# The tile that two attention heads share: three operand pairs for its scores where there were four, with copies inside SBUF

## The chip, the cores and the metric

The kernel runs on one core of a Trainium2 chip. The metric is the device time of one execution, in microseconds (us). The engines are named as in the profile: PE multiplies matrices (PEld is its loading of the stationary operand), DVE, ACT and POOL work on elements, and SP only issues transfers, which the core's DMA engines then carry out.

## The reference, cut to what matters

Three layers follow one another. The first is attention over 16 heads (2 batches of 8) of 1152 keys and 64 features; the queries are averaged in pairs, so a head has 576 of them:

```python
q_pool = q.reshape(B, H, S // 2, 2, D).mean(axis=3)
scores = scale * q_pool @ k.T
attn = softmax(scores)          # over the 1152 keys
x = attn @ v
```

Two feed-forward layers come after it (512 to 2048 to 512 with ELU; an RMS norm, and 512 to 1536 to 512 with SwiGLU). The change touches only the scores of the first layer.

## The kernel before, in words

All matrix products are made in a type that keeps fewer bits than float32, so every operand is split in an upper part (the value rounded to that type) and a lower part (what the rounding left), and a product is a sum over such parts. For the scores this is laid out along the 128 rows that a product sums over. A head has 64 features. Its keys are in a tile `kd` of 128 x 1152: rows 0 to 63 hold the upper parts of the 64 features, rows 64 to 127 the lower parts (`prep_k`, L248). Its queries are in a tile `qt` of 128 x 2 x 704: plane 0 has the upper parts, in both halves of the rows, plane 1 the lower parts, in both halves too (`prep_q`, L236). So plane 0 times `kd` gives upper times (upper plus lower), and plane 1 times `kd` gives lower times (upper plus lower). The first and last 64 columns of `qt` are zeros.

The heads are worked in 8 pairs, p = 0 to 7, with j = 0 and 1 in a pair. A head's 576 queries are four tiles of 128 and a rest of 64. The rests of both heads make one shared tile, number 2 (`M`) in the list `TILES`, so that a pair has nine tiles. In the shared tile the first 64 output rows belong to one head and the last 64 to the other, and the zero columns of `qt` keep the heads apart.

The loop over `steps` has 72 steps, one for each tile: `emit_S` (L268) makes the scores in PSUM (tile `s`, one buffer of three banks, each written by products of 384 columns) and DVE reads them once (L283) into `p`, with their extreme; `do_T` transposes the tile of two steps ago on PE (L297), with ACT (L305) and DVE (L69) splitting the result into `pth` and `ptl`; `do_AV` runs eight products with the values (L323); `emit_exp` is on ACT (L288). A full tile takes 2 operand pairs x 3 banks = 6 score products, the shared tile 4 x 3 = 12. The order within a pair is the list's, so the shared tile is the third; only pair 0 has it fifth.

Each engine works through its instructions in the order in which the program gives them, and so does SP's queue of transfers. Behind the exponent a step has up to one preparing job for the heads of the next pair (`plan`, L401): a job waits for a raw load (`load`, L221, tiles `rawq`, one buffer, and `rawk` and `rawv`, two buffers together), and POOL adds the query pairs, rounds and subtracts (L243, L60, L63). When a job is emitted, the load for the job after it is put in SP's queue (`fetch`, L396). In pair 0 ACT does some of the rounding (L389). In the last 33 steps a step also puts out one operation on the weights of the next layer (`ws.step`, L500), whose loads (L90) are in SP's queue too. POOL also joins the halves of the output (L339) and spreads the softmax sums (`rs`).

Of the kernel before, what the change touches and what calls it, by code (L numbers as in the profile page):

```python
# [9 lines left out]
F32R = mybir.dt.float32r  # L10
# [8 lines left out]
S = 1152  # L19
# [19 lines left out]
def tile_kernel(ctx: ExitStack, tc: tile.TileContext, qd, kd, vd, w1d, w2d, wgd, wvd, wod, rgd, outd):  # L39
    nc = tc.nc  # L40
    V, G, T, PE, SP = nc.vector, nc.gpsimd, nc.scalar, nc.tensor, nc.sync
    ctx.enter_context(tc.manual_schedule())
    f = lambda a: a.bitcast(F32)
# [29 lines left out]
    class Stream:  # L73
# [10 lines left out]
        def load(self, n):  # L84
            while self.loaded < min(n, len(self.srcs)):
                i = self.loaded
                t = wp.tile([128, 512, 2], U32, tag="wr", name="wr", bufs=2)
                r = t.rearrange("p c w -> p (c w)")
                if wide:
                    SP.dma_start(out=r, in_=self.srcs[i].bitcast(U32))  # L90
                else:
                    t = f(r)[:, 0:512]
                    SP.dma_start(out=t, in_=self.srcs[i])
                self.raw[i] = t
                self.loaded += 1
# [103 lines left out]
    ap = actx.enter_context(tc.tile_pool(name="attn", bufs=1))  # L199
# [19 lines left out]
    KD, VD, QD = {}, {}, {}  # L219
# [28 lines left out]
    def prep_k(p, j, half, t, eng):  # L248
# [4 lines left out]
        hi(d, t)  # L253
        lo(d[64:128], t[64:128], d[64:128])

    def prep_v(p, j, t, eng):
        hi, lo = eng
        d = VD[p, j] = ap.tile([128, 9, 128], F32R, tag="vd", name="vd", bufs=3)
        hi(d[:, :, 0:64], t)
        lo(d[:, :, 64:128], t, d[:, :, 0:64])  # L260
# [7 lines left out]
    def emit_S(p, i):  # L268
        if i == 0:
            st[p] = ap.tile([128, 4, NPT, 1], F32, tag="st", name="st", bufs=2)  # L270
        s = (tp if (p, i) == (0, 1) else sp).tile([128, 3, 512], F32, tag="s", name="s", bufs=1)
        if i == M:
            parts = [(QD[p, j][:, u, c:c + 128], KD[p, j]) for j, c in ((1, 0), (0, 576)) for u in (0, 1)]
        else:
            j, c, _, _, _ = TILES[i]
            parts = [(QD[p, j][:, u, c:c + 128], KD[p, j]) for u in (0, 1)]
        for n, (a, b) in enumerate(parts):
            for m in range(3):
                PE.matmul(s[:, m, 0:384], lhsT=a, rhs=b[:, 384 * m:384 * m + 384],  # L279
                          start=n == 0, stop=n == len(parts) - 1)  # L280
        pt = P[p, i] = ap.tile([128, 3, 384], F32, tag="p", name="p", bufs=3)

        V.tensor_scalar(out=pt, in0=s[:, :, 0:384], scalar1=-0.0625, scalar2=None,  # L283
                        op0=ALU.mult, op1=ALU.min, accum_out=st[p][:, 0, TILES[i][4], :])

    def emit_exp(p, i):
        pt = P[p, i]
        T.activation(out=pt, in_=pt, func=AF.Exp, scale=-1.0, bias=st[p][:, 0, TILES[i][4], :],  # L288
                     accum_out=st[p][:, 1, TILES[i][4], :])
# [57 lines left out]
    def emit_r(p):  # L347
        s = st[p]
        V.tensor_scalar(out=s[:, 2], in0=s[:, 1], scalar1=1e-9, scalar2=None, op0=ALU.add)
        V.reciprocal(s[:, 3], s[:, 2])  # L350
        hi_pool(rs, s[:, 3, 0:8].to_broadcast([128, 8, 64]))

    def emit_scale(p):

        s, x = st[p], xf[p]
        rb, rm = tbank(), tbank()
        for k in range(4):
            PE.transpose(rb[:, 128 * k:128 * k + 128], rs[:, 2 * k:2 * k + 2, :].rearrange("p a b -> p (a b)"), ident)
        PE.transpose(rm[:, 0:128], s[:, 3, 8, :].to_broadcast([128, 128]), ident)
        xs = ap.tile([128, QS], F32, tag="xs", name="xs", bufs=1)  # L360
        for a, b in ((0, 0), (320, 256)):
            T.copy(xs[:, a:a + 256], rb[:, b:b + 256])
        for j in range(2):
            r = slice(64 * j, 64 * j + 64)
            T.copy(xs[r, 256:320], rm[r, r])
        return xs

    def emit_x(p, xs, a=0, b=QS):
        x = xf[p][:, a:b]
        n, c = divmod(p, 4)  # L370
        h, l = (t[:, c, n * QS + a:n * QS + b] for t in (xh, xl))
        if p < 7:
            G.tensor_tensor(out=x, in0=x, in1=xs[:, a:b], op=ALU.mult)
            hi_pool(h, x)
            lo_pool(l, x, h)
        else:
            V.tensor_tensor(out=x, in0=x, in1=xs[:, a:b], op=ALU.mult)
            T.copy(h, x)
            lo_dve(l, x, h)
# [11 lines left out]
    def do_prep(u, eng):  # L391
        {"q": prep_q, "k": prep_k, "v": prep_v}[u[0]](*u[1:], raws.pop(u), eng)
# [3 lines left out]
    def fetch(u):  # L396
        if u not in raws:
            raws[u] = load(*u)


    plan = {1: lambda p: ("v", p, 0), 2: lambda p: ("q", p + 1, 1), 3: lambda p: ("k", p + 1, 1, 0),  # L401
            4: lambda p: ("k", p + 1, 1, 1), 5: lambda p: ("v", p + 1, 1), 6: lambda p: ("q", p + 1, 0),
            7: lambda p: ("k", p + 1, 0, 0), 8: lambda p: ("k", p + 1, 0, 1)}
    steps = [(p, i) for p in range(8) for i in ([0, 1, 3, 4, 2, 5, 6, 7, 8] if p == 0 else range(NPT))]
    ns = len(steps)
    jobs = {n: [] for n in range(-1, ns)}
    for n in range(ns):
        p, k = n // NPT, n % NPT
        if p == 0:
            u = {0: [("k", 0, 0, 1)], 2: [("v", 0, 1)], 3: [("v", 0, 0)]}.get(k, [])  # L410
            jobs[n] += u
        if k in plan and not (p == 0 and k == 1):
            u = plan[k](p)
# [36 lines left out]
    def do_T(step):  # L450
        pt, it = steps[step - LT]
        if avq and any(overwrites(it, a.g) for a in avq):
            assert not any(overwrites(it, a.g) for a in avq[1:])
            avq[0].emit(18)
        emit_T(pt, it)

    def do_AV(k, then):
        while k and avq:
            k -= avq[0].emit(k)
            if avq[0].n < 18:  # L460
                break
            a = avq.pop(0)
            a.finish()
            if a.g is GROUPS[3]:
                then(a.p)

    def after_T(step):
        pt, it = steps[step - LT]
        seen.add((pt, it))
        for g in GROUPS:  # L470
            if it in g["tiles"] and all((pt, t) in seen for t in g["tiles"]):
                avq.append(AV(pt, g))

    for step in range(ns):
        emit_S(*steps[step])
        if step == 1:
            tctx.close()
            tp = actx.enter_context(tc.tile_pool(name="psT", bufs=1, space=PSUM))
            tbank = lambda: tp.tile([128, 512], F32, tag="t", name="t", bufs=3)

        due = [w for w in later if w[0] <= step]
        if step >= LT and not due:
            do_T(step)
        for w in due:
            later.remove(w)
            w[1]()
        do_AV(8, lambda p: later.append((step + 2, lambda: emit_x(p, emit_scale(p)))))
        if step >= LT and due:
            do_T(step)
        emit_exp(*steps[step])  # L490
        if step >= LT:
            if steps[step - LT][1] == NPT - 1:
                emit_r(steps[step - LT][0])
            after_T(step)
        for u in jobs.get(step, []):
            do_prep(u, (ACT[0], lo_pool) if step < 4 and u[0] != "q" else POOL)
            n = order.index(u)
            if n + 1 < len(order):
                fetch(order[n + 1])
        ws.step(0, step >= ns - 33)  # L500


# [87 lines left out]
    for hf in range(2):  # L590
# [28 lines left out]
        if hf:  # L619
            T.activation(out=dummy, in_=eps, func=AF.Sqrt)  # L620
            for c in range(3):
                for n in range(4):
                    m, q = 2 + n // 2, n % 2
# [113 lines left out]
```

## Time and profile before

| | us |
|---|---|
| median of 3 runs | 697.13 (696.63 to 697.89) |
| the profiled execution: its own time | 696.5 |
| the profiled execution: span from first to last instruction | 694.7 |
| attention within the span | about 0 to 257 |
| PE busy, of the span | 680.0 (98%) |
| DVE busy | 538.2 (77%) |
| ACT busy | 415.0 (60%) |
| POOL busy | 372.6 (54%) |

The span is what the trace shows, and the execution's own time lies 1.8 us above it. Busy shares are means over stages of different make: in attention all five engines are used hard, in the two later layers PE above all. PE's busy time counts products that overlap each other, so 98% doesn't say that PE works at its peak.

### The profile page before, as it was taken

What the parts mean: (1) busy time and instruction counts of PE and PEld (TensorE: products, weight loads), DVE (VectorE), ACT (ScalarE), POOL (GpSimd) and SP (SyncE); (2) the same over time, 40 slices, a digit from 0 to 9 for tenths busy, and PEclk for the clock granted to TensorE, in tenths of its full rate; (3) what the DMA queues carried; (4) which work ended last, traced back from release to release, by engine and by line L of the source; (5) the groups of instructions that cost most, each with busy time, mean ns of one, the idle gap of its engine ahead of it and who ended that gap; (6) DMA issues with size and microseconds to landing.
All of it is one profiled execution on the core that took longest, in us unless ns stands there. A gap on an engine that the chain in (4) does not pass through costs nothing.

```text
span 694.7 us, 11366 instructions
## 1 busy us (share of the span) xinstructions
PE 680.0 (98%) x4243; PEld 668.1 (96%) x4243; DVE 538.2 (77%) x891; ACT 415.0 (60%) x855; POOL 372.6 (54%) x332
## 2 busy tenths in 40 slices
PE   7999999999999999999999999799999999999998
PEld 6999999989898999999999999799999999999997
DVE  6888889898999877999959999866999876584000
ACT  5888889789888857774447764334444443342000
POOL 5988788897978405674434544532554343342000
PEclk9999999999999999999999999999999999999999
DMA  5423323432432000213422123201323222232000
GB/s 181 144 86 113 128 87 103 144 119 87 134 129 72 1 31 32 92 60 129 145 92 85 67 86 127 91 1 38 116 92 121 92 97 92 87 106 80 35 35 34
DMA packets 21607, 62.34 MB, mean 90 GB/s; under 512 B 2736, under 2 KB 4784, under 8 KB 21552
## 3 DMA queue, kind: packets, MB, share of 16 engines
q1 hardware_dynamic: 21552, 61.62, 26.2%
q8 instruction: 33, 0.54, 0.3%
q14 instruction: 22, 0.18, 0.1%
HBM read 59.25 MB, written 2.36 MB: 89 GB/s over the span
## 4 chain that ended last, share of the span: by engine, by line
PE 78%; DVE 15%; ACT 4%; issue 1%; DVEq 0%; ACTq 0%
PE b L167 16%; PE b L169 16%; PE b L168 16%; PE s L279 10%; PE o L323 9%; PE t L297 8%; DVE p L283 3%; DVE ptl L69 2%; DVE wt L124 2%; DVE wt L128 2%; DVE wt L120 1%; DVE gl L69 1%; DVE e L187 1%; DVE wt L122 1%; ACT gh L188 1%
## 5 line engine op out<-in xcount | busy, mean ns | idle before, releaser
L167 PE MATMUL b<-xh,wh 128*128 128x384 f32 x468 | 157.3, 336 | 0.6 <-ACT sl L638 0.6
L169 PE MATMUL b<-xh,wl 128*128 128x384 f32 x468 | 157.1, 336 | 0.0
L168 PE MATMUL b<-xl,wh 128*128 128x384 f32 x468 | 157.0, 335 | 0.0
L63 POOL TENSOR_TENSOR wl<-wt,wh 128x512 fp32r<-128x512 f32 x68 | 98.4, 1447 | 76.6 <-ACT wh L141 48.2
L283 DVE TENSOR_SCALAR_CACHE_REDUCE p<-s 128x1152 f32<-128x1152 f32 x72 | 97.4, 1354 | 21.1 <-PE s L279 20.7
L69 DVE TENSOR_TENSOR ptl<-t,pth 128x384 fp32r<-128x384 f32 x216 | 106.7, 549 | 3.5 <-ACT pth L305 3.0
L279 PE MATMUL s<-kd,qt 128*128 128x384 f32 x480 | 98.0, 341 | 5.6 <-DVE p L283 4.6
L305 ACT CAST pth<-t 128x384 fp32r<-128x384 f32 x216 | 89.3, 486 | 23.1 <-PE t L297 22.5
L288 ACT ACTIVATE p<-p,st 128x1152 f32<-128x1152 f32 x72 | 91.4, 1269 | 5.2 <-DVE p L283 4.9
L279 PEld LDWEIGHTS s<-kd,qt 128*128 128x128 f32 x480 | 81.5, 188 | 9.0 <-DVE p L283 4.0
L167 PEld LDWEIGHTS b<-xh,wh 128*128 128x128 f32 x468 | 87.9, 188 | 0.9 <-ACT sl L638 0.9
L168 PEld LDWEIGHTS b<-xl,wh 128*128 128x128 f32 x468 | 87.9, 188 | 0.0
L169 PEld LDWEIGHTS b<-xh,wl 128*128 128x128 f32 x468 | 87.9, 188 | 0.0
L297 PE MATMUL t<-ident,p 128*128 128x128 f32 x648 | 85.9, 275 | 0.0
L323 PE MATMUL o<-pth,vd 128*128 128x256 f32 (+1 forms) x288 | 84.4, 315 | 0.0
L297 PEld LDWEIGHTS t<-ident,p 128*128 128x128 f32 x648 | 73.9, 141 | 6.8 <-DVE ptl L69 4.3
L323 PE MATMUL o<-ptl,vd 128*128 128x256 f32 (+1 forms) x288 | 78.4, 295 | 0.0
L113 ACT ACTIVATE wt<-wr 128x512 f32<-128x512 f32 x68 | 45.7, 672 | 51.2 <-POOL wl L63 31.8
L124 DVE SCALAR_TENSOR_TENSOR wt<-wr,wt 128x512 uint32<-128x512 uint32 x68 | 73.2, 1076 | 1.4
L128 DVE CUSTOM_DVE_ANT_0 wt<-wt,we 128x1024 uint16<-128x1024 uint16 x68 | 66.7, 981 | 1.9
L63 POOL TENSOR_TENSOR gl<-e,gh 128x384 fp32r<-128x384 f32 x37 | 40.2, 1087 | 44.5 <-ACT gh L188 42.8
L167 PE MATMUL b<-gh,wh 128*128 128x384 f32 x180 | 61.5, 342 | 0.0
(113 smaller groups left out, 1321.3 us busy)
## 6 DMA issues: line engine op xcount, KB each, us to landing
wr<-in_w_dram SPq DMA_DIRECT2D x32, 512.0 KB, 3.2
rawk<-in_k_dram SPq DMA_DIRECT2D x32, 288.0 KB, 2.9
rawq<-in_q_dram SPq DMA_DIRECT2D x15, 576.0 KB, 3.9
wr<-in_wg_dram SPq DMA_DIRECT2D x12, 512.0 KB, 3.2
wr<-in_wv_dram SPq DMA_DIRECT2D x12, 512.0 KB, 3.2
wr<-in_wo_dram SPq DMA_DIRECT2D x12, 512.0 KB, 3.2
rawv<-in_v_dram SPq DMA_DIRECT2D x16, 288.0 KB, 2.8
out_dram<-o SPq DMA_DIRECT2D x12, 192.0 KB, 1.8
```

The costliest lines, as they stand in the source:

```text
L63: G.tensor_tensor(out=o, in0=i, in1=f(h), op=ALU.subtract)
L69: V.tensor_tensor(out=o, in0=i, in1=f(h), op=ALU.subtract)
L124: V.scalar_tensor_tensor(out=t, in0=hi, scalar=0x80000000, in1=t, op0=ALU.bitwise_and, op1=ALU.bitwise_xor)
L167: PE.matmul(out, lhsT=wh[:, k, :], rhs=ah, start=first and k == 0, stop=False)
L168: PE.matmul(out, lhsT=wh[:, k, :], rhs=al, start=False, stop=False)
L169: PE.matmul(out, lhsT=wl[:, k, :], rhs=ah, start=False, stop=last and k == 3)
L279: PE.matmul(s[:, m, 0:384], lhsT=a, rhs=b[:, 384 * m:384 * m + 384], start=n == 0, stop=n == len(parts) - 1)
L283: V.tensor_scalar(out=pt, in0=s[:, :, 0:384], scalar1=-0.0625, scalar2=None, op0=ALU.mult, op1=ALU.min, accum_out=st[p][:, 0, TILES[i][4], :])
L288: T.activation(out=pt, in_=pt, func=AF.Exp, scale=-1.0, bias=st[p][:, 0, TILES[i][4], :], accum_out=st[p][:, 1, TILES[i][4], :])
L297: PE.transpose(ps[:, k, :], src[:, 128 * b:128 * b + 128], ident)
L305: T.copy(oh, re(ps))
L323: PE.matmul(self.o[:, 0:self.N], lhsT=v[:, b, :], rhs=(pth, ptl)[u][:, g["buf"], b, g["c0"]:320], start=self.n == 0, stop=self.n == 17)
```

## The change

For the shared tile, the two products with the lower parts of the queries, one for each head, become one. A new stationary tile `qm` (128 x 128) is block-diagonal: rows and columns 0 to 63 hold the lower parts of head 0's 64 queries, rows and columns 64 to 127 those of head 1's; the rest is set to zero once. A new moving tile `km` (128 x 1152) has the upper parts of head 0's keys in rows 0 to 63 and those of head 1's in rows 64 to 127. The shared tile then has three operand pairs, and nine products; the products of lower parts with lower parts are no longer in it.

`qm` and `km` have one buffer each and are filled for each pair by four transfers inside SBUF in SP's queue (`prep_m`): a 64 x 64 block into `qm` and 64 x 1152 into `km`, for either head. They are put out behind the job that prepares head 0's queries for the next pair (for pair 0, behind that of the second half of head 0's keys). The order of the jobs is changed: head 0's keys go to steps 5 and 6, its queries to step 7, and head 1's values from step 5 to step 8.

```diff
+    qm = ap.tile([128, 128], F32R, name="qm")
+    km = ap.tile([128, S], F32R, name="km")
+    V.memset(f(qm), 0.0)
+
+    def prep_m(p):
+        for j, c in ((0, 576), (1, 64)):
+            r = slice(64 * j, 64 * j + 64)
+            SP.dma_start(out=f(qm[r, r]), in_=f(QD[p, j][r, 1, c:c + 64]))
+            SP.dma_start(out=f(km[r]), in_=f(KD[p, j][0:64]))
...
         if i == M:
-            parts = [(QD[p, j][:, u, c:c + 128], KD[p, j]) for j, c in ((1, 0), (0, 576)) for u in (0, 1)]
+            parts = [*((QD[p, j][:, 0, c:c + 128], KD[p, j]) for j, c in ((1, 0), (0, 576))), (qm, km)]
...
     plan = {1: lambda p: ("v", p, 0), 2: lambda p: ("q", p + 1, 1), 3: lambda p: ("k", p + 1, 1, 0),
-            4: lambda p: ("k", p + 1, 1, 1), 5: lambda p: ("v", p + 1, 1), 6: lambda p: ("q", p + 1, 0),
-            7: lambda p: ("k", p + 1, 0, 0), 8: lambda p: ("k", p + 1, 0, 1)}
+            4: lambda p: ("k", p + 1, 1, 1), 5: lambda p: ("k", p + 1, 0, 0), 6: lambda p: ("k", p + 1, 0, 1),
+            7: lambda p: ("q", p + 1, 0), 8: lambda p: ("v", p + 1, 1)}
...
             if n + 1 < len(order):
                 fetch(order[n + 1])
+            if u == ("k", 0, 0, 1) or u[0] == "q" and u[2] == 0:
+                prep_m(u[1])
         ws.step(0, step >= ns - 33)
```

## Rows read from the trace of the kernel before

**Rows 1.** The page, busy time by engine, and the chain that ended last.
```profile
PE 680.0 (98%) x4243; PEld 668.1 (96%) x4243; DVE 538.2 (77%) x891; ACT 415.0 (60%) x855; POOL 372.6 (54%) x332
...
PE 78%; DVE 15%; ACT 4%; issue 1%; DVEq 0%; ACTq 0%
```

**Rows 2.** Windows: stretch, length, then each engine's busy us, clock, DMA share, GB/s.
```profile
70.00:100.00 30.00, 30.00 (x221) 29.22 (x220) 25.98 (x51) 25.70 (x56) 25.28 (x25) 1.00 0.33 108
...
192.40:224.00 31.60, 30.44 (x220) 29.18 (x219) 29.69 (x55) 26.86 (x58) 27.43 (x25) 1.00 0.29 94
```

**Rows 3.** Chain of waits in order of time, pair 2's shared tile (start, us).
```profile
70.05 2.11 PE s L279 x12
```

**Rows 4.** DVE's timeline in pair 6 (start, us, instruction, idle before it and releaser).
```profile
194.72 1.36 DVE L283 TENSOR_SCALAR_CACHE_REDUCE p<-s 128x1152 f32<-128x1152 f32 x1 [0.58 <-PE s L279]
...
200.95 1.36 DVE L283 TENSOR_SCALAR_CACHE_REDUCE p<-s 128x1152 f32<-128x1152 f32 x1 [0.21 <-PE s L279]
```

**Rows 5.** POOL's timeline: the opening, the passage to pair 2, and that to pair 6.
```profile
13.11 1.42 POOL L63 TENSOR_TENSOR qt<-rawq,qt 128x576 fp32r<-128x576 f32 x1
14.61 2.77 POOL L63 TENSOR_TENSOR kd<-rawk,kd 64x576 fp32r<-64x576 f32 x2
...
18.86 1.42 POOL L243 TENSOR_TENSOR rawq<-rawq 128x576 f32<-128x576 f32 x1
...
69.13 0.88 POOL L339 TENSOR_TENSOR xf<-xf,olo 64x320 f32<-64x320 f32 x1
...
71.79 0.67 POOL L60 TENSOR_SCALAR vd<-rawv 128x576 fp32r<-128x576 f32 x1
72.54 1.42 POOL L63 TENSOR_TENSOR vd<-rawv,vd 128x576 fp32r<-128x576 f32 x1
75.02 0.87 POOL L339 TENSOR_TENSOR xf<-xf,olo 64x320 f32<-64x320 f32 x1 [1.05 <-ACT xf L338]
...
191.00 0.90 POOL L339 TENSOR_TENSOR xf<-xf,olo 64x320 f32<-64x320 f32 x1
```

**Rows 6.** PE's timeline: the shared tile's products in pairs 0, 2 and 6.
```profile
17.07 2.32 PE L279 MATMUL s<-kd,qt 128*128 128x384 f32 x12 [0.82 <-DVE p L283]
...
69.89 2.27 PE L279 MATMUL s<-kd,qt 128*128 128x384 f32 x12
...
192.41 2.27 PE L279 MATMUL s<-kd,qt 128*128 128x384 f32 x12
```

**Rows 7.** SP's queue: transfers issued in the opening and before pair 2.
```profile
14.56 0.33 SPq L224 DMA_DIRECT2D rawq<-in_q_dram  x1
14.98 0.39 SPq L233 DMA_DIRECT2D rawv<-in_v_dram  x1
...
66.92 0.33 SPq L233 DMA_DIRECT2D rawv<-in_v_dram  x1
67.30 0.42 SPq L224 DMA_DIRECT2D rawq<-in_q_dram  x1
```

**Rows 8.** The page, transfers (count, KB each, median us from issue to landing).
```profile
rawk<-in_k_dram SPq DMA_DIRECT2D x32, 288.0 KB, 2.9
...
out_dram<-o SPq DMA_DIRECT2D x12, 192.0 KB, 1.8
```

**Rows 9.** Transfers issued between 13.5 and 22 us, columns as in rows 8.
```profile
rawq<-in_q_dram SPq DMA_DIRECT2D x1, 576.0 KB, 4.0
rawv<-in_v_dram SPq DMA_DIRECT2D x1, 288.0 KB, 4.3
```

**Rows 10.** ACT's timeline in pair 0.
```profile
11.86 0.66 ACT L389 CAST kd<-rawk 128x576 fp32r<-128x576 f32 x1
...
19.34 0.67 ACT L389 CAST vd<-rawv 128x576 fp32r<-128x576 f32 x1 [0.27 <-DMA rawv<-in_v_dram]
...
22.71 1.24 ACT L305 CAST pth<-t 128x384 fp32r<-128x384 f32 x3 [0.31 <-PE t L297]
...
25.68 0.48 ACT L305 CAST pth<-t 128x384 fp32r<-128x384 f32 x1 [0.48 <-PE t L297]
```

## The prediction

> **What bounds the kernel now.** I read the page first: PE is busy for 98% of the span, and 78% of the chain that ended last lies on PE, 15% on DVE [rows 1]. A mean over three layers can't tell what a saving in the first is worth, so I took the windows of single pairs of heads next. [...] The chain of waits shows the change's place: the shared tile's twelve score products stand on it as one piece of 2.11 us, 0.176 each [rows 3]. In the late pairs the question is whether DVE could use scores that come sooner. It can: in pair 6 it idled 0.58 us before it read the shared tile's scores and still 0.21 us two tiles later, both times for PE [rows 4]. [...] Last I read POOL, SP and PE beside each other at the passage from one pair to the next, since the new operand hangs on all three.
>
> **The removed products.** Three of 0.176 us leave each shared tile: 0.53 us a pair, 4.2 us over eight pairs, if nothing else is late. The time for three more weight loads goes with them. The zeroing of `qm` is one DVE instruction in the first microseconds, when DVE waits for the first load; its price is nothing, and if that cover were gone, some tenths once.
>
> **When the new operand is there.** It is copied when POOL has the lower parts of head 0's queries. The new order ends with that job and then head 1's values, so it is done one values job before the jobs end. In the passage to pair 2 they end at 69.13, where the addition follows them, and a values job lasts from 71.79 to 73.96, 2.17 us [rows 5]; the queries are then ready at 66.96. For pair 6 the same is 191.00 - 2.17 = 188.83. That all jobs together end where they did is my reading: each load still goes out when its buffer comes free, and POOL's idle 1.05 us before the next addition [rows 5] takes up small shifts. This wait is for a result behind the shared tile, so POOL keeps its distance from PE, and the distance below stays as it is when the tile gets shorter.
>
> **When it is wanted.** The shared tile began at 69.89 in pair 2 and at 192.41 in pair 6 [rows 6]. The two upper-part products on three banks come first, 6 x 0.176 = 1.06 us, so `qm` and `km` are wanted at 70.95 and 193.47. From POOL's end that leaves 3.99 us in pair 2 and 4.64 in pair 6. The four copies have that long to be issued and to land.
>
> **What the copies need.** SP issued two transfers 0.38 us apart [rows 7], so the fourth goes out 1.14 us after the first. No transfer from SBUF to SBUF stands in the trace. Below is the store from SBUF, 192 KB in 1.8 us; beside it the key load of the very size of one `km` half, 288 KB in 2.9 us [rows 8]; above, the slowest load of that size that I show, 4.3 us, issued behind twice its bytes [rows 9]. So the last copy has landed 2.94, 4.04 or 5.44 us after POOL's end. I take 4.04, the load of the same bytes, since the copy shares its queue with another as large. It misses pair 2 by 0.05 us and no later pair. Pairs 2 to 7 then give 6 x 0.53 - 0.05 = 3.1 us.
>
> [...] The trace has no 64-row transfer. [...]
>
> **What waits behind the copies.** SP's queue is in order: behind the waiting first copy stand the loads of head 0's values and of the next queries, and in late pairs one weight load. From pair 2 on those values go out some 1.5 us later than at 66.92 [rows 7], land near 72, and POOL wants them at 71.79; the 1.05 us idle before the addition [rows 5] hides that. Without this cover it would be some tenths a pair. The weight load is used a whole pair later.
>
> **The opening pays.** In pair 0 the first copy waits for the lower parts of head 0's queries, ready at 14.53 [rows 5]. The shared tile starts at 17.07 [rows 6] and wants the operand at 18.13; 14.53 + 4.04 is 18.57, a stall of 0.44, which I see covered by what follows. The four copies push two loads 4 x 0.38 = 1.52 us back: queries from 14.56 and values from 14.98 [rows 7]. These took 4.0 and 4.3 us [rows 9] and have no slack. POOL took up the queries at 18.86 [rows 5], 0.3 after they landed, so its chain of jobs moves by 1.2 us. ACT stood waiting for the values at 19.34 [rows 10], so its cast and all behind it, first the transposes' casts, come 1.5 us late. ACT's idle 0.31 and 0.48 us before its next groups of casts [rows 10] give back 0.8, and I let PE lose the other 0.7, with pair 0's own saving inside that. In pair 1 the operand comes 1.2 + 4.04 after the old end of POOL's work, and is wanted 3.99 (pair 2's figure stands in) + 0.7 after it: a stall of 0.55, against the 0.53 saved. Opening: a loss of 0.7 us.
>
> **Sum.** 3.1 - 0.7 = 2.4 us faster. The profiled execution took 696.5 us by itself, and would take 694.1; the median of the runs is 0.6 us above that execution, so I say 694.7. With the store's price there is no stall: the opening is +0.2, the sum -3.0. With the slowest load's, the six later pairs stall 1.45 to 0.80 us each, some 6.6 in all against 3.2 saved, and the opening costs about 3.5 (copies and loads 1.4 later still): +6.9.
>
> **Rivals.** A difference of 0.2% (1.4 us) is about what can be told from no change.
>
> *The copies are late in every pair.* PE waits before the last three products of each shared tile, with every score behind it. It decides from a landing of about 4.9 us: pair 2 then stalls 0.9 and pair 6 0.3, which together eat nearly all of the saving, and the opening's loss of some 2 us remains. The time is 698.6 at that point and 704 at 5.44. [...] Against it: stores from SBUF landed fastest of all [rows 8]. Chance 0.16.
>
> *The opening is dearer.* If the copy of head 0's keys also waits for their lower parts, which POOL finishes at 14.61 + 2.77 = 17.38 [rows 5] and which the copied rows 0 to 63 don't hold, everything in the opening moves another 2.85 us: about +0.4, 697.5. Less of the same comes if ACT's idle gives nothing back (0.8 us). Against it: the copied rows are written by ACT alone, and were done at 11.86 + 0.66 [rows 10]. Chance 0.16.
>
> *DVE takes the saving in the late pairs.* If its lead there absorbs 0.53 us in each of pairs 4 to 7, 2.1 us go: 696.8. Its idle in rows 4 speaks against it. Chance 0.08.
>
> *The opening is free.* The loads slip into idle time and all eight savings stay: 693.1. Chance 0.10.
>
> The forecast, 693.9 to 695.7, has the remaining 0.50. Faster than 695.7 are nearly all of it and the free opening: 0.57. Within 1.4 us either way are the dear opening, DVE's case and the forecast's upper edge: 0.27. Slower: 0.16. The range from 692.9 to 698.6 leaves out most of the late copies and a little below.
>
> **What would show it.** In the changed kernel's trace: 456 score products; shared tiles as one piece near 1.58 us in pairs 2 to 7, without a wait on a DMA inside; the time between the starts of two shared tiles near 29.3 us in pairs 2 and 3; a last copy landing about 4 us after POOL's subtraction; ACT's cast of the values in pair 0 waiting until near 20.8; and the two later layers unchanged. A wait of PE for `km` over 0.5 us in the middle pairs would make the prediction wrong, and so would an opening more than 2 us later.

## The result: 9.7 us slower, and the profile after

The median of four runs of the changed kernel was 706.86 us (705.61 to 708.04), beside 697.11 (696.63 to 697.89) for the kernel before on the same chip: a ratio of 1.014, 95% interval 1.0128 to 1.0152. The prediction was 694.7 with a range up to 698.6, so both the sign and the range were wrong. The profiled execution's span grew from 694.7 to 704.2 us. The mean granted clock was 0.997 in both.

In the changed kernel all line numbers behind the new function are 12 higher: the score products are L291, DVE's reading L295, the transposes L309, POOL's addition L351. The copies are L265 (`qm`) and L266 (`km`). From its page, against [rows 1] and [rows 8]:

```profile
PE 678.3 (96%) x4219; PEld 663.6 (94%) x4219; DVE 539.6 (77%) x892; ACT 414.5 (59%) x855; POOL 374.3 (53%) x332
...
PE 64%; POOL 12%; DVE 9%; DMA 6%; ACT 4%; issue 2%; SPq 2%; POOLq 0%; DVEq 0%; ACTq 0%
...
rawv<-in_v_dram SPq DMA_DIRECT2D x16, 288.0 KB, 3.6
km<-kd SPq DMA_DIRECT2D x16, 288.0 KB, 3.5
```

The 24 removed products are gone (4243 to 4219). But the chain that ended last is on PE for 64% of the span instead of 78%; POOL, the transfers and SP's queue now stand on it. Its list of waits (engine, line, waited for; us in total, times, longest) says where:

```profile
POOL vd L60 <- DMA rawv<-in_v_dram: 15.6, 7, 3.6
...
PE s L291 <- DMA km<-kd: 10.6, 7, 2.5
```

Here is the passage to pair 2, which the prediction worked through. First the chain of waits in order of time (start, us), then PE's timeline at the shared tile, then POOL's, all of the changed kernel:

```profile
69.12 1.44 POOL qt L63
70.56 0.02 issue
70.57 0.47 SPq L265
71.04 0.05 issue
71.09 0.59 SPq L266
71.68 0.05 issue
71.73 0.59 SPq L265
72.32 0.04 issue
72.36 3.46 DMA km<-kd
75.82 0.14 issue
75.96 0.76 PE s L291 x3
```

```profile
73.84 1.23 PE L291 MATMUL s<-kd,qt 128*128 128x384 f32 x6
75.96 0.76 PE L291 MATMUL s<-km,qm 128*128 128x384 f32 x3 [0.89 <-DMA km<-kd]
```

```profile
76.90 0.67 POOL L60 TENSOR_SCALAR vd<-rawv 128x576 fp32r<-128x576 f32 x1 [1.13 <-DMA rawv<-in_v_dram]
```

POOL has the queries at 70.56; PE can use the operand at 75.96, 5.40 us later. The upper-part products ended at 73.84 + 1.23 = 75.07, so PE stood 0.89 us. It did so in every pair: 1.43, 2.54, 0.89, 1.00, 1.07, 1.44, 1.59 and 1.59 us in pairs 0 to 7, 11.55 in all (the list of waits books one of the eight as "issue"), where the removed products were to save 4.2. The shared tile began at 73.84 in pair 2 and at 198.85 in pair 6, against 69.89 and 192.41 [rows 6]: the loss grows through attention, by 3.95 us up to pair 2, 6.44 up to pair 6, and 9.5 at the end of the span.

### The profile page after: what moved, and what is told of

It reads as the page before. It is cut to its first block, busy times and chain, and to the rows that moved or that the text cites. A ratio compares the mean times of both kernels' runs of the same rounds, so it can differ in the third digit from the quotient of the medians.

```text
span 704.2 us, 11401 instructions
## 1 busy us (share of the span) xinstructions
PE 678.3 (96%) x4219; PEld 663.6 (94%) x4219; DVE 539.6 (77%) x892; ACT 414.5 (59%) x855; POOL 374.3 (53%) x332
## 3 DMA queue, kind: packets, MB, share of 16 engines
q1 hardware_dynamic: 24112, 66.60, 29.3%
## 4 chain that ended last, share of the span: by engine, by line
PE 64%; POOL 12%; DVE 9%; DMA 6%; ACT 4%; issue 2%; SPq 2%; POOLq 0%; DVEq 0%; ACTq 0%
PE b L167 16%; PE b L169 16%; PE b L168 16%; PE o L335 5%; PE s L291 5%; PE t L309 5%; POOL kd L63 3%; POOL rawq L243 2%; POOL qt L63 2%; DMA km<-kd 2%; DVE wt L128 2%; DMA rawv<-in_v_dram 1%; DVE wt L124 1%; DVE wt L120 1%; DMA rawq<-in_q_dram 1%
## 5 line engine op out<-in xcount | busy, mean ns | idle before, releaser
L295 DVE TENSOR_SCALAR_CACHE_REDUCE p<-s 128x1152 f32<-128x1152 f32 x72 | 97.3, 1353 | 29.4 <-PE s L291 27.6
L291 PE MATMUL s<-kd,qt 128*128 128x384 f32 x432 | 89.9, 343 | 4.3 <-DVE p L295 3.9
L309 PE MATMUL t<-ident,p 128*128 128x128 f32 x648 | 85.9, 275 | 0.9 <-DVE ptl L69 0.7
L309 PEld LDWEIGHTS t<-ident,p 128*128 128x128 f32 x648 | 73.8, 141 | 8.1 <-DVE ptl L69 5.2
L291 PEld LDWEIGHTS s<-kd,qt 128*128 128x128 f32 x432 | 73.0, 188 | 7.9 <-DVE p L295 2.8
L128 DVE CUSTOM_DVE_ANT_0 wt<-wt,we 128x1024 uint16<-128x1024 uint16 x68 | 68.7, 1010 | 1.9
```

What stands on the lines that cost most here:

```text
L128: V.tensor_tensor(out=t, in0=t, in1=e, op=ALU.add)
L309: PE.transpose(ps[:, k, :], src[:, 128 * b:128 * b + 128], ident)
```

## Two loops that the copies close

The rows suggest two theories, which are not exclusive. **Loop A**: POOL's queries, copies, PE's last three products, everything on PE behind them up to the next transposed sums, ACT's copies of these, POOL's jobs behind them, and the next queries. If the copies are late once they stay late, since POOL starts its next jobs later by as much. **Loop B**: POOL's queries, copies, and in SP's queue behind them the load of head 0's values, for which POOL waits, then POOL's jobs and the next queries. The rivals: the traffic itself, the changed order of the jobs, and the opening alone.

## The experiments

Every kernel has the new order of jobs. The times of the kernel before in the same sessions were 696.79 to 696.97 us.

**Nothing copied.** `qm` and `km` are zeroed once; nine products a shared tile.

```diff
+    V.memset(f(km), 0.0)
-            if u == ("k", 0, 0, 1) or u[0] == "q" and u[2] == 0:
-                prep_m(u[1])
```

> The changed kernel without its four copies: the stacked tiles are zeroed once and never filled, so the shared tile's third operand pair is zeros and the product of lower query parts with upper key parts is left out; nine products and the new order of jobs stay. Theory A (the copies land too late, PE waits for them): without them the saving of 0.53 us a pair comes through, 4.2 us: about 693. Theory B (the loads behind the copies are late): the same, 693, since nothing stands in the queue. Rival C (the three products are worth nothing, because DVE or POOL sets the pace, or the new order of jobs costs the time): 696 to 700.

Measured: 691.16 us, ratio 0.9918 (0.9901 to 0.9934). **The order alone**, in the kernel before:

> The kernel before with the new order of jobs alone. Theories A and B: no change, 696.5 to 697.5. Rival C (the order itself costs): 699 or more.

Measured: 694.78 us, ratio 0.9969 (0.9957 to 0.9981). So the order costs nothing. It gains 2.1 us, which I had not expected (last section), and the three removed products bring another 3.6 of the 4.2 us. (These are differences of medians of four to six runs; the 95% intervals leave about 1 us on each.) The copies and what hangs on them cost 706.86 - 691.16 = 15.7 us.

**Copies made, never read.** The shared tile keeps its four operand pairs and twelve products, so loop A is cut.

```diff
-            parts = [*((QD[p, j][:, 0, c:c + 128], KD[p, j]) for j, c in ((1, 0), (0, 576))), (qm, km)]
+            parts = [(QD[p, j][:, u, c:c + 128], KD[p, j]) for j, c in ((1, 0), (0, 576)) for u in (0, 1)]
```

> The changed kernel with the four copies issued as before, but the shared tile made of the old four operand pairs, twelve products, which read none of the copies; the output is complete. Theory A alone: PE has nothing to wait for, so only the opening loses: 697 to 699. Theory B: POOL still waits for the values that are loaded behind the copies, and its loop from one query job to the next stays above PE's 29.8 us a pair, as in the changed kernel (30.5 in the early pairs, near 33 in the late ones): 700 to 704.

Measured: 704.96 us, ratio 1.0121 (1.0104 to 1.0138): 10.2 us above the order alone, although PE waits for no copy. But the loss is not spread over the pairs. The shared tiles start at 42.68, 72.55, 102.41 and 132.28, PE's old 29.87 apart, and the next only at 169.16, 36.88 later. Against the order alone the tile is 2.1 us late in pair 1 (42.68 against 40.59), which is the opening, and 8.1 in pair 5 (169.16 against 161.04). What went on meanwhile is on POOL (the first two rows below, pairs 1 and 2), in the chain of waits (pair 4) and on ACT:

```profile
47.64 0.67 POOL L60 TENSOR_SCALAR vd<-rawv 128x576 fp32r<-128x576 f32 x1 [2.50 <-DMA rawv<-in_v_dram]
...
78.58 0.67 POOL L60 TENSOR_SCALAR vd<-rawv 128x576 fp32r<-128x576 f32 x1 [3.52 <-DMA rawv<-in_v_dram]
```

```profile
135.28 3.62 DMA rawv<-in_v_dram
...
139.81 1.44 POOL vd L63
141.25 0.02 issue
141.26 0.33 SPq L230
141.59 0.05 issue
141.64 3.86 DMA wr<-in_w_dram
```

```profile
145.52 0.67 ACT L113 ACTIVATE wt<-wr 128x512 f32<-128x512 f32 x1 [4.58 <-DMA wr<-in_w_dram]
```

POOL waits 2.5 to 3.5 us for head 0's values in each of pairs 1 to 4. Its head 0 queries end at 40.98, 71.25, 102.29 and 132.62, 2.0 us more than PE's three periods of 29.87; POOL drifts behind PE without stopping it. In pair 4 the bill comes: a load of keys can't be issued until POOL frees its buffer at 141.25, the first loads of the next layer's weights stand behind it in SP's queue, ACT waits 4.58 us for them, and the casts of the transposes stand behind that. PE stood 3.44 us for them until 147.20; from about 148.5 to 151.5 the granted clock was then 0.50 (0.992 as the mean of the run), and six score products at 150.71 took 1.52 us on the chain, where 1.05 is usual, so a part of the 6 us lost here is the clock's. Loop B is real, but it hurts in one place and through a third party.

**Copies behind the values.** From pair 1 on the copies are put out one job later, so loop B is cut and loop A stays.

```diff
-            if u == ("k", 0, 0, 1) or u[0] == "q" and u[2] == 0:
+            if u == ("k", 0, 0, 1) or u[0] == "v" and u[2] == 1 and u[1] > 0:
```

> The changed kernel with the copies for pairs 1 to 7 put out one job later, behind the load of the next pair's first values; in SP's queue that load then goes ahead of them. Theory A: POOL's waits for values shrink, but the copies still land 5.4 us after the query job, so PE still waits 0.8 to 1.4 us a pair: 702 to 705. Theory B alone: with the values in time the loss is gone in pairs 2 to 7 and only the opening's remains: 697 to 700.

Measured: 706.11 us, ratio 1.0134 (1.0119 to 1.0149). POOL's wait for head 0's values is gone from the list; it now waits for what comes after the shared tile. From the waits and the chain of that kernel:

```profile
POOL xf L351 <- ACT xf L350: 16.4, 7, 4.8
PE s L291 <- DMA km<-kd: 11.5, 8, 2.9
```

```profile
73.14 0.47 SPq L265
...
74.93 3.46 DMA km<-kd
...
78.53 0.76 PE s L291 x3
...
90.42 1.04 PE s L291 x6
91.46 0.45 PE t L370 x4
...
91.94 0.60 ACT xs L374 x2
...
94.11 1.43 POOL xf L385
...
102.31 1.44 POOL qt L63
103.77 0.47 SPq L265
```

That is loop A, whole: from one issue of the copies to the next 103.77 - 73.14 = 30.63 us, where PE's own work needs 29.3. In this profiled run PE's wait of 2.88 us in pair 1 was also followed by a granted clock of 0.50, from about 46.5 to 49.5 us, and the next pair came 32.05 us later; in the changed kernel's attention the granted clock stayed at 1.00.

**Both loops cut**: copies behind the values, and unread.

> The copies are put out behind the load of the values (from pair 1 on) and nothing reads them; the shared tile has the old four operand pairs and the output is complete. Theory (there are two loops, copies to PE to POOL and copies to the values' load to POOL, and either alone sets the pace): with both cut the time is that of the new order alone (694.8) plus what pair 0's copies cost in the opening: 695 to 698.5, and the middle pairs are 29.9 us apart. Rival (the traffic inside SBUF or the room that the copies take in SP's queue costs by itself): 702 to 706 as in the kernels with one loop cut, pairs over 30.4 apart.

Measured: 696.89 us, ratio 1.0001 (0.9992 to 1.0011), middle pairs 29.84 to 29.87 apart. The same 32 issues and as many bytes of copies as in the changed kernel are there, and 2.1 us are lost against the order alone, 1.6 of them by pair 1 (42.15 against 40.59). So apart from these 2.1 us neither the traffic nor its room in the queue is the cause; what waits for them is. Loop B alone costs 10.2 us (704.96 over the order alone), loop A alone 15.0 (706.11 over the kernel that copies nothing), both 15.7, each with the opening in it. They don't add up, and 15.0 and 15.7 can hardly be told apart. My reading, which no run shows, is that who waits in the one loop finds the other's result there.

**The opening.** Copies for pair 0 alone:

```diff
-            if u == ("k", 0, 0, 1) or u[0] == "q" and u[2] == 0:
+            if u == ("k", 0, 0, 1):
```

> The changed kernel with copies for pair 0 alone; the shared tiles of pairs 1 to 7 read pair 0's operand, so their part from the lower query parts is another pair's. Theory (the opening's loss is a few us at most, the rest of the loss comes from pairs 1 to 7): 691.2, the time without any copy, plus 1.5 to 3.5 us: 692.7 to 694.7; middle pairs 29.3 us apart. Rival (the opening is where most of it goes): 698 to 704.

Measured: 693.13 us, ratio 0.9949 (0.9934 to 0.9964). Over 691.16 that is 2.0 us for the opening.

**Copies of 128 rows.** The same bytes, number and places, but each `km` copy takes 128 rows of 576 columns.

```diff
-            SP.dma_start(out=f(km[r]), in_=f(KD[p, j][0:64]))
+            h = slice(QS * j, QS * j + QS)
+            SP.dma_start(out=f(km[:, h]), in_=f(KD[p, j][:, h]))
```

> The changed kernel with each copy of 64 rows by 1152 columns into the moving tile replaced by one of 128 rows by 576 columns: the same number of transfers, bytes and places in the queue. The tile then holds other parts of the keys than it should, which the output shows. If the 64 rows make the copies slow (the rate during them was about 200 GB/s where loads of 128 rows have 400), the last copy lands 2.2 to 2.6 us after its issue in place of 3.5, PE's wait shrinks to 0 to 0.6 us a pair and the values behind the copies come a microsecond earlier: 697 to 702. Rival (copies inside SBUF are slow whatever their rows, or the issue cost is all): landing stays at 3.5, 706 to 707.

Measured: 702.59 us, ratio 1.0088 (1.0075 to 1.0102), 4.3 below the changed kernel. From its page:

```profile
rawv<-in_v_dram SPq DMA_DIRECT2D x16, 288.0 KB, 3.2
km<-kd SPq DMA_DIRECT2D x16, 288.0 KB, 2.5
```

The copies land in 2.5 us in place of 3.5, and the waits for them nearly vanish in pairs 2 to 5 (the shared tiles' last products 29.4 apart from pair 2 to 4). The rate is in the window of transfers from 69.5 to 80 us of the changed kernel, 40 slices of 0.26 us (tenths of the 16 engines' time, then GB/s; the last `km` copy landed at 75.82, in slice 25):

```profile
DMA  0000000020579959899977889999999997200000
GB/s 0 0 0 0 0 0 0 0 57 6 123 176 263 193 105 263 210 239 193 263 140 149 237 298 395 439 413 439 386 439 369 369 404 281 80 0 0 0 0 0
```

While the copies are under way the engines are as busy as later, yet move some 200 GB/s; the loads behind them move 370 to 440. The 128-row copies reached 369 to 403 (window 69 to 77 us of their kernel). So the copies of 64 rows moved at about half the rate of those of 128 rows. That is part of the lateness, not all: 702.59 is still a loss. What is left lies elsewhere: pair 5 comes 32.2 us after pair 4, and PE waits 2.31 and 0.65 us for the copies in pair 7. The edit also lets the first of the three products go with the first copy alone (in pair 0 it starts 0.73 us ahead of the other two); in pairs 2 to 5 all three run as one piece, without a wait.

**Off the path: early key copies.** The upper key parts need not wait for the queries. Here each head's `km` copy stands behind the job of its second key half, and POOL writes the two 64 x 64 blocks of `qm` itself.

```diff
+    def prep_km(p, j):
+        r = slice(64 * j, 64 * j + 64)
+        SP.dma_start(out=f(km[r]), in_=f(KD[p, j][0:64]))
+    def prep_qm(p, j):
+        r, c = slice(64 * j, 64 * j + 64), (576, 64)[j]
+        hi_pool(qm[r, r], f(QD[p, j][r, 1, c:c + 64]))
...
+    prep_km(0, 1)
+    prep_qm(0, 1)
...
+    prep_qm(0, 0)
...
+            if u[0] == "k" and u[3] == 1:
+                prep_km(*u[1:3])
+            if u[0] == "q":
+                prep_qm(*u[1:3])
```

> A version meant to keep the saving: the key copies are put out behind the job of the second half of each head's keys, one to four steps earlier than now, and POOL itself writes the 64 x 64 blocks of the queries (rows stay in place, so no transfer is needed), about 0.25 us each. Both loops (through PE's wait, through the values behind the copies) hang on the copies standing behind the query job; if they are the whole loss, this comes near the kernel without copies: 691 to 693.5. Rival (the traffic of the copies, or POOL's two further instructions, cost by themselves): 695 to 699.

Measured: 698.87 us, ratio 1.0032 (1.0019 to 1.0044). From pair 1 on it is near what was wished: the last products at 49.18, 78.48, 107.82 and 137.18, 29.3 apart, no wait. The loss is in one place, pair 0. It has its shared tile fifth, and by then the program has written pair 1's block into `qm`. From the timelines of PE and POOL:

```profile
13.66 2.18 PE L311 MATMUL t<-ident,p 128*128 128x128 f32 x9 [2.71 <-ACT p L302]
...
23.89 1.33 PE L293 MATMUL s<-km,qm 128*128 128x384 f32 x3 [3.12 <-POOL qm L60]
```

```profile
23.59 0.24 POOL L60 TENSOR_SCALAR qm<-qt 64x64 fp32r<-64x64 f32 x1
```

In this kernel and the next, pair 0's tile therefore takes one block of pair 1, and waits for it. That isn't all. PE had already stood 2.71 us, because ACT waited 5.56 us for head 0's keys (its cast came at 11.69, against 9.53 in the changed kernel), now with a `km` copy issued behind their load. And the granted clock was 0.50 from about 13 to 19.7 us and from 23.5 to 29.5 us, from the end of each wait on (0.988 as the mean of the run, 0.997 in the changed kernel): the nine transposes at 13.66 took 2.18 us, where 1.14 is usual. How the loss splits between these was not tested. **The same with SP's transfers for the blocks:**

```diff
-        hi_pool(qm[r, r], f(QD[p, j][r, 1, c:c + 64]))
+        SP.dma_start(out=f(qm[r, r]), in_=f(QD[p, j][r, 1, c:c + 64]))
```

> As the run with early key copies, but the two 64 x 64 query blocks stay transfers in SP's queue behind the query jobs, 16 KB each. They need one issue and about 2.3 us to land, 2.9 after POOL's end, against some 4 us that PE leaves; the values stand behind one transfer of 0.5 us in place of four. If what counts is what stands behind the query job, this is within 1 us of the other: 691 to 694. Rival (any transfer behind that job closes the loops): 699 or more.

Measured: 713.0 us, ratio 1.0238 (1.0221 to 1.0255). The wait in pair 0 is 7.38 us, with a granted clock of 0.50 for some 16 of the first 34 us (0.983 as the mean of the run). And a transfer of 16 KB that waits for POOL holds up the key loads in SP's queue: POOL waited 17.3 us for them in all. Most of the rest is in one place again, from pair 4 to 5, 38.81 us apart, where ACT waited up to 6.4 us for weights, as with the unread copies. So the small transfers that wait cost no less here than the large ones (706.86 us).

**Pair 0 left as it was**, the rest as where POOL writes the blocks, without the calls in the opening:

```diff
+            parts = [(QD[p, j][:, u, c:c + 128], KD[p, j]) for j, c in ((1, 0), (0, 576)) for u in (0, 1)]
+            if p > 0:
+                parts = [*((QD[p, j][:, 0, c:c + 128], KD[p, j]) for j, c in ((1, 0), (0, 576))), (qm, km)]
...
+            if u[0] == "k" and u[3] == 1 and u[1] > 0:
+            if u[0] == "q" and u[1] > 0:
```

> As the kernel with early key copies and POOL's own writing of the query blocks, but pair 0's shared tile keeps the four old operand pairs and needs no copy. Theory (the new operand is worth its three products where its copies stand in nobody's way, and what that kernel lost was pair 0's tile alone): the opening is that of the kernel before with the new order, shared tiles 29.3 us apart in the middle pairs, and the time is near that of the kernel with nine products and no copies (691.2): 691 to 692.7, faster than the kernel before by 0.6 to 0.9%. Rival (the copies and POOL's two small operations a pair still cost what the three products save): 694 to 696, the time of the new order alone. Second rival: over 697, then the early key copies hold up SP's queue in the late pairs too.

Measured: 692.1 us (691.75 to 692.42), ratio 0.9926 (0.9914 to 0.9939): 4.9 us faster than the kernel before and 14.8 faster than the changed one. Its copies still take 3.3 us to land. SP's queue and the shared tile of pair 2:

```profile
53.52 0.47 SPq L264 DMA_DIRECT2D km<-kd  x1
...
62.38 0.47 SPq L264 DMA_DIRECT2D km<-kd  x1
```

```profile
71.32 0.68 PE L295 MATMUL s<-km,qm 128*128 128x384 f32 x3
```

The second copy is issued 8.9 us before its use. This kernel lies 0.9 us above the one that copies nothing, which is no more than such differences leave open. In the traces its last products come 0.3 us later in pair 1 (41.99 against 41.70) and 1.4 later in pair 7 (222.07 against 220.69), so most of that arises in the pairs that carry weights; its cause was not tested.

## Why the prediction was wrong

**What bounds the kernel, and what the products are worth: right.** PE set the pace of the middle pairs [rows 2], and nine products bring 3.6 us over the order alone, against 4.2; pairs come 29.3 us apart without the copies.

**"What the copies need" failed.** I took 4.04 us from POOL's end and forecast from that; 5.40 was measured, next to my upper bound of 5.44, which is luck, since that bound's 4.3 was the price of a load of values behind twice its bytes [rows 9]. The parts: the fourth copy went out 1.80 us after POOL's end (72.36), where I had 1.14 from a spacing of 0.38 between two loads [rows 7]; behind one another the copies are issued about 0.6 us apart. It landed after 3.46 us, where I had 2.9 from a 128-row load [rows 8]. And 0.14 passed before PE used it. The slack was 4.51 us in pair 2 (75.07 - 70.56), more than my 3.99, but short of 5.40. The forecast priced a copy of 64 rows by a load of 128, since the trace had no 64-row transfer; with 128 rows the copies landed 1.0 us sooner.

**The rival "the copies are late in every pair" is what happened**, given 0.16. Its working at 5.44 was +6.9, with stalls of 6.6 in pairs 2 to 7 and 3.5 in the opening; measured were 7.58 and, up to pair 2's shared tile, 3.95, and +9.5 in all. It missed that the stalls don't shrink in late pairs. In pair 6 POOL's end fell 2.6 us before the shared tile's start (196.26 to 198.85), where I had 3.6 from the kernel before. The step that failed there is "When the new operand is there": with the new order alone, and no copy, the distance is already 2.9 us in pair 2 (67.57 to 70.46), as I had it, but 2.8 in pair 6 (189.28 to 192.09). The jobs together don't end where they did.

**"What waits behind the copies" failed.** I let 1.05 us of POOL's idle hide the values. They were issued at 73.20 and taken up at 76.90 with a wait of 1.13 in pair 2, and 3.60 in pair 6:

```profile
204.40 0.67 POOL L60 TENSOR_SCALAR vd<-rawv 128x576 fp32r<-128x576 f32 x1 [3.60 <-DMA rawv<-in_v_dram]
```

In pair 6 a weight load stands between the copies and the values, which I had called harmless because it is used a pair later. That looks at the load itself, not at what stands behind it. With the copies unread this step alone cost 10.2 us, opening included; outside the opening I had put it at nothing. The changed kernel's last two pairs are 32.7 and 33.4 us apart, against 32.3 in both with loop A alone; how the rest splits between the loops the runs don't say, since each hides the other.

**"The opening pays" had the right sign and a third of the size**: 2.0 us against 0.7. The queries' load went out 2.0 us later than before (I had 1.52), POOL took them up 2.2 later (against 18.86 [rows 5]), ACT's cast of the values came 2.4 later (against 19.34 [rows 10]), and PE waited 1.43 us for the operand where I saw 0.44. SP's queue, POOL's and ACT's timelines in the changed kernel's opening:

```profile
16.56 0.58 SPq L224 DMA_DIRECT2D rawq<-in_q_dram  x1
```

```profile
21.07 1.45 POOL L243 TENSOR_TENSOR rawq<-rawq 128x576 f32<-128x576 f32 x1 [2.91 <-DMA rawq<-in_q_dram]
```

```profile
21.78 0.68 ACT L401 CAST vd<-rawv 128x576 fp32r<-128x576 f32 x1 [3.21 <-DMA rawv<-in_v_dram]
```

The rival by which the copy of keys waits for their lower parts is out: both `km` copies were issued by 15.68, before POOL's end with those parts at 13.87 + 2.78 = 16.65.

**DVE did not take the saving** in the late pairs: without copies these are 30.5 us apart, against 31.0 with the order alone.

## What to carry to other kernels

A transfer that waited for a result held up what stood behind it in SP's queue (POOL waited 2.5 to 3.5 us for the values behind the unread copies), so its price here was the lateness of the loads behind it, not its own bytes: 10.2 us ahead of the values, 2.1 behind them. And a result that came late into a loop of engines stayed late (30.63 us round the loop, 29.3 on PE): compare the loop's whole length with the period, not one slack with one landing. Where an operand has a part that is ready early, send that part early (8.9 us ahead here), and leave the small late part to the engine that makes it (0.24 us a block on POOL).

## What the runs showed of the hardware that was not expected

The order alone gained 2.1 us by the medians (0.9 between the two profiled spans, with 0.5 lost in the opening). The gain is in the pairs that carry weights: their shared tiles come 30.85, 31.05 and 31.02 us apart, where it was 31.25, 31.61 and 31.63. Part of it stands on DVE. One of its operations on the weights, with two inputs in SBUF, took 1.37 us in pairs 5 and 6 of the kernel before, beside POOL's addition of queries, and 0.68 with the new order, when POOL prepares keys. From DVE's timelines, first of the kernel before, then of the order alone:

```profile
182.83 1.37 DVE L124 SCALAR_TENSOR_TENSOR wt<-wr,wt 128x512 uint32<-128x512 uint32 x1
```

```profile
183.20 0.68 DVE L124 SCALAR_TENSOR_TENSOR wt<-wr,wt 128x512 uint32<-128x512 uint32 x1
```

The difference is 0.69 us each time. On POOL, too, an operation beside it took longer in both: its rounding of the queries 0.99 and 1.00 us in the kernel before, where 0.67 is usual, its subtraction for the keys 1.79 in the new order, where 1.43 is usual. That this makes the whole gain was not tested.

Transfers inside SBUF: 288 KB over 64 rows landed in 3.5 us, over 128 rows in 2.5, and a block of 16 KB still took 2.3 in the changed kernel. In a row, four were issued 0.5 to 0.8 us each, where a load issued by itself took 0.33.

The granted clock fell to 0.50 for about 3 us after waits of PE of 2.88 us (copies behind the values, pair 1) and 3.44 us (copies unread, pair 4); nine transposes then took 2.04 us (on PE's timeline, where 1.14 is usual) and 1.80 us (on the chain, where 0.98 is usual). In the kernel before, behind attention, it was 0.50 from about 451 to 454.5 us, after waits of 1.6 and 2.1 us, and products of 384 columns came 0.32 us apart there instead of 0.17. So such a wait seems to cost more than its own length; no run separates the two.
